# First-tile weight chunks kept whole beside their halves, and the first V remainders summed on TensorE

## The chip, the core and the metric

One core of one Trainium2 chip runs the whole program. The metric is device time in microseconds (us) per execution. Engines in the profile: PE is TensorE (PEld its weight loads), DVE is VectorE, ACT is ScalarE, POOL is GpSimd, SP is the queue from which every DMA is issued.

## The reference

Attention over pooled keys and values, then two feed-forward layers one after the other, all in float32.

```python
k_p = k.reshape(B, H, Sp, pool, D).mean(axis=3)      # B, H, S, D = 8, 8, 576, 64; pool 8, Sp 72
v_p = v.reshape(B, H, Sp, pool, D).mean(axis=3)
scores = (1 / sqrt(D)) * matmul(q, k_p^T);  attn = softmax(scores)
x = matmul(attn, v_p)  ->  [4608, 512]
h = x @ w_in;   y = maximum(0.01 * h, h) @ w_out                  # layer 1, d_ff 2048
h = y @ w_in2;  out = (h * clip(h + 3, 0, 6) / 6) @ w_out2        # layer 2, d_ff 2048
```

## The kernel before

**Attention** goes in units: of each of the 8 batches b, two units of 4 heads over the first 384 tokens, and one of all 8 heads over the last 192. Unit n of batch 0 is u0, u1, u2; batch 1 begins with unit 3. A unit is, in this order: pooled sums of K and V (`prep_k`, `prep_v`, DVE), scores on TensorE (`scores`, L525 for u0 and u1, L541 for the rest), the softmax (DVE maximum L578, exponentials on ACT L602, or, where the half's number stands in the list `sub`, a subtraction on DVE L587 and one exponential L591; then the sum, its reciprocal L614, the remainder L627 and the normalisation L652 on DVE), transposes on TensorE (L678, and L695 for the remainder, the last 8 of 72 pooled keys), and the products with V (`values`, L717 and L729). For u0 and u1 the V sums are made on TensorE by eight accumulating products with the identity (`pool_v`, L451); the sums of the V remainder (`u.r` into `u.rs`) are reductions on DVE (`sum_pool`, L426).

**Layers.** Each float32 operand is split into a rounded high part and a low rest, and a product is three matmuls (hi*hi, hi*lo, lo*hi). Tokens 0 to 383 are one tile of width 384, tokens 384 to 895 one of width 512; the remaining tokens go in pairs of tiles with seven Strassen-like products per pair instead of eight (`Pair1`, `Pair`, TensorE line L1167). The work on TensorE runs in this order: attention u0 to u2, tile 0 with the first 8 of 16 weight chunks (L905 to L907 and L949 to L951, width 384), tile 1 with all 16 (same lines, width 512), tile 0 with the last 8 chunks (width 384), and then the pairs, with the other attention units strewn in between.

**Weights** of layer 1 come as packed words. `decode` (L829, L835 on ACT, L838 on DVE) makes a float32 chunk, a copy its high part, a subtraction (L347) its low part. In tile 0 `decode_w` decodes into scratch that the next chunk overwrites; only the two parts remain. The pairs need sums and differences of quarters of each pair of chunks (`combine`), so `first_weights(f)` adds the high and low parts of chunks 2f and 2f+1 up again with four DVE additions of 128x512 (`plus(part, hi, lo, 512)`, L1032) and then combines. `pair_weights`, for the chunks 8 to 15, keeps the decoded chunk whole and combines from it.

**Order.** `Plan.order` is a list scheduler: every instruction has an engine (some copies may go to ACT or DVE: the first `flex` tasks), an estimated cost and the tasks it depends on; a pass from the end gives each a rank, and each engine takes the ready task of the lowest rank. The result is written out as the fixed order of every queue. The table `C` sets the slots at which attention units (`att...`, `gaps...`), weight steps (`when...`, `left...`) and preparations (`prep...`) are handed to it. Where the plan leaves TensorE a gap ahead of the first second product of tile 0 (`fill_until`), it writes products with zeros into it (`idle`, L1654).

Of the kernel before, what the change touches and what calls it, by code (L numbers as in the profile page):

```python
# [21 lines left out]
POOL, SP = 8, 72  # L22
# [11 lines left out]
    soon={0: 0, 1: 1200, 2: 800, 4: 1000, 3: 9000, 5: 12000, 7: 3000, 6: 5500},  # L34
    flex=684,
    mid=8,
    halves=13,
    sub=[1, 2, 3, 10, 13, 20, 23, 27, 29, 30, 32, 43],
    parts=24,
    when0=[0, 0, 0, 0, 4, 1, 12],  # L40
    att0=[0, 4, 8],
    gaps0=[0, 0, 1, 2, 0],
    when1=[4, 8, 13, 26],
    att1=[0, 4, 16, 22, 40],
    gaps1=[0, 3, 3, 3, 0],
    att2=[1],
    gaps2=[0, 3, 10, 13, 27],
    prep2=[126, 111],
    att=[[16, 26, 33, 49], [12, 26, 41, 60, 76], [1, 18, 47, 60], []],
    gaps=[[0, 3, 7, 10, 0], [0, 10, 13, 13, 8], [0, 0, 7, 12, 0], [198, 0, 80, 79, 49]],  # L50
    prep3=[107, 239],
    prep=[[102, 207], [155, 105], [189, 154], [92, 151]],
    left1=[[[0, 127], [1, 47]], [[2, 10], [3, 54]]],
    left2=[[], [], [[0, 44]], [[1, 30], [2, 51]], [[3, 7], [4, 27]], [[5, 25], [6, 34]], [[7, 6]]],
# [222 lines left out]
def attention_moe_moe(ctx: ExitStack, tc: tile.TileContext, qt, kt, vm, vr, wt, wq, eye, mask, out):  # L277
# [83 lines left out]
    vp = {}  # L361
# [83 lines left out]
    def pool_v(u):  # L445

        u.vs = buf("h", [128, 512], F32, 2, psum)(None, lambda t: t[:, 0:128])

        def emit():
            for i in range(POOL):  # L450
                PE.matmul(  # L451
                    out=u.vs.ap(), lhsT=ident.ap(), rhs=u.v.ap()[:, i * 128 : i * 128 + 128], start=i == 0, stop=i == POOL - 1
                )

        on_pe(1860, emit, [u.v, ident], [u.vs])
# [21 lines left out]
    def prep_v(u):  # L477
        if u.b == 1:
            vp[u.g] = buf(f"vp{u.g}", [128, 128])()
        held_values[u.g] = u.b  # L480
        if u.early:
            pool_v(u)
            copy(whole_v[u.g], u.vs, 128, True)
        else:
            whole_v[u.g] = vp[u.g]
            sum_pool(whole_v[u.g], u.v, 128)
        sum_pool(u.rs, u.r, 64)
# [181 lines left out]
    def transposes(u):  # L669
# [11 lines left out]
        for pi, ps in enumerate(pss):  # L681
            src = ps(None, lambda t: t[:, 0:HALF])
            dst = u.wide_t[pi] if u.b == 0 else buf("th", [128, HALF], F32, 2)()
# [160 lines left out]

    def decode_w(f, raw, t, l, halves=False):

        wf = buf(f"w{f}", [128, 4, 512], F32R)
        w[f] = wf
        for h in range(2) if halves else (None,):
            if h is None:  # L850
                th, lh, n = t, l, 1024
                hi, lo = [wf(what, lambda t, a=a: t[:, a : a + 2].rearrange("p a n -> p (a n)")) for what, a in (("hi", 0), ("lo", 2))]
            else:
                th, lh = [part(v, h, lambda t, h=h: t[:, 512 * h : 512 * h + 512]) for v in (t, l)]
                hi, lo, n = *[wf((what, h), lambda t, a=a: t[:, a]) for what, a in (("hi", h), ("lo", 2 + h))], 512
            decode(raw, th, lh, h)
            copy(hi, th, n)
            subtract(lo, th, hi, n)
        keep(f, wf)
# [217 lines left out]

    def first_weights(f):

        t = new_raw()  # L1080
        for i in range(2):
            for g in range(2):

                dst = [t((i, j) if g == 0 else (j, i)) for j in range(2)]

                def cut(v, i=i, g=g):
                    at = v.rearrange("p (i j g n) -> p i j g n", i=2, j=2, g=2)
                    return at[:, i, :, 0, :] if g == 0 else at[:, :, i, 1, :]

                wf = w[2 * f + i]  # L1090
                hi, lo = [
# [6 lines left out]
    def pair_weights(f):  # L1098
# [3 lines left out]
        for i in range(2):  # L1102
# [13 lines left out]
            for g in range(2):  # L1116
                decode(words, part[g], new_st()(None, lambda t: t[:, 0, :]), g)
# [595 lines left out]
```

## Time and profile before

| | |
|---|---|
| median of 3 runs | 1523.93 us (1522.87 to 1524.26) |
| profiled execution | 1524.98 us, of which the span from first to last instruction is 1522.9 us |
| TensorE | 1514.3 us busy, 99% of the span, 8697 matmuls |
| VectorE, ScalarE | 1152.8 us and 965.2 us busy |
| products with zeros | 225 |

A busy TensorE in the profile also counts products with zeros, and matmuls that run at the lower clock; so the busy share alone does not show what is lost. Starts of neighbouring matmuls tell more than their durations, since they overlap.

### The profile page before, as it was taken

The page shows a single profiled execution, that of the slowest core. Times are in us where ns is not written, and L with a number is a line of the kernel's source. Part 1 is how long each engine was busy: PE and PEld are TensorE (multiplying, and loading weights), DVE is VectorE, ACT ScalarE, POOL GpSimd, SP SyncE. Part 2 cuts the span into 40 slices and gives each one's busy share as a digit, 9 for nine tenths or more (in the row PEclk, how much of TensorE's full clock was granted, in tenths as well). Part 3 has the DMA queues.
Part 4 walks back from the last instruction along what each step waited for, and adds up shares of the span by engine and source line. Part 5 has one row for each costly group of instructions (what it writes and reads, how often), then busy time and mean ns, then how long its engine had stood idle before and what let it go on. Part 6 is the DMA issues. An engine that isn't in the chain of part 4 may idle for free.

```text
span 1522.9 us, 24498 instructions
## 1 busy us (share of the span) xinstructions
PE 1514.3 (99%) x8697; PEld 1318.0 (87%) x8697; DVE 1152.8 (76%) x2054; ACT 965.2 (63%) x2138; POOL 2.5 (0%) x10
## 2 busy tenths in 40 slices
PE   9999999999999999999999999999999999999999
PEld 8877889998787888988888888888888888999999
DVE  8998986788589875975697769657855785596685
ACT  7888567766777777666666556545544554565554
POOL 0000000000000000000000000000000000000000
PEclk9999999999999999999999999999999999999999
DMA  9999899999998999999987966755675567778775
GB/s 323 329 350 321 300 321 324 315 330 343 336 311 323 313 337 325 324 319 337 328 293 258 338 200 206 278 194 208 234 237 195 209 226 246 255 263 299 251 268 197
DMA packets 143209, 432.64 MB, mean 284 GB/s; under 512 B 14960, under 2 KB 51440, under 8 KB 124912
## 3 DMA queue, kind: packets, MB, share of 16 engines
q1 hardware_dynamic: 143088, 431.09, 82.0%
q8 instruction: 69, 1.13, 0.3%
q14 instruction: 52, 0.43, 0.1%
HBM read 345.05 MB, written 85.98 MB: 283 GB/s over the span
## 4 chain that ended last, share of the span: by engine, by line
PE 95%; DVE 3%; ACT 1%; DMA 1%; issue 0%; SPq 0%; DVEq 0%; ACTq 0%
PE y L1167 45%; PE h L1167 24%; PE a L1167 12%; PE y L949 2%; PE y L951 1%; PE y L950 1%; PE h L905 1%; PE h L907 1%; PE h L906 1%; PE a L541 1%; PE a L729 1%; PE a L678 1%; PE idle L1654 1%; PE a L717 1%; DMA x<-x 1%; PE a L695 0%
## 5 line engine op out<-in xcount | busy, mean ns | idle before, releaser
L1032 DVE TENSOR_TENSOR w<-y,w 128x512 f32<-128x512 f32 (+2 forms) x124 | 78.7, 638 | 120.1 <-PE y L1167 118.2
L340 ACT ACTIVATE gh<-w 128x512 fp32r<-128x512 f32 (+1 forms) x140 | 82.3, 589 | 63.8 <-PE y L1167 25.4
L1167 PE MATMUL y<-w,xh 128*128 128x512 f32 (+2 forms) x552 | 121.0, 370 | 0.6 <-DMA xh<-left 0.6
L1032 DVE TENSOR_TENSOR w<-w 128x512 f32<-128x512 f32 (+2 forms) x184 | 113.8, 640 | 3.9 <-ACT w L923 3.6
L1167 PEld LDWEIGHTS y<-w,xh 128*128 128x128 f32 x552 | 100.6, 188 | 15.4 <-issue 1.2
L337 ACT CAST gh<-w 128x512 fp32r<-128x512 f32 (+2 forms) x128 | 74.6, 584 | 49.0 <-PE y L1167 24.7
L1365 DVE SCALAR_TENSOR_TENSOR gl<-w,gh 128x512 fp32r<-128x512 f32 (+1 forms) x140 | 89.4, 641 | 19.3 <-ACT gh L340 19.1
L347 DVE TENSOR_TENSOR gl<-w,gh 128x512 fp32r<-128x512 f32 (+2 forms) x128 | 82.0, 640 | 21.2 <-ACT gh L337 20.7
L1167 PE MATMUL y<-w,xl 128*128 128x512 f32 (+2 forms) x408 | 91.2, 371 | 0.0
L1167 PEld LDWEIGHTS y<-w,xl 128*128 128x128 f32 x408 | 74.6, 188 | 10.6 <-issue 1.2
L1336 ACT ACTIVATE gh<-w,three 128x512 f32<-128x512 f32 (+1 forms) x60 | 40.9, 681 | 66.5 <-DVE w L1032 66.5
L347 DVE TENSOR_TENSOR w<-x,w 128x512 fp32r<-128x512 f32 (+2 forms) x108 | 67.6, 637 | 19.5 <-ACT w L337 19.5
L923 ACT ACTIVATE w<-w 128x512 f32<-128x512 f32 (+2 forms) x96 | 56.1, 595 | 38.3 <-DVE w L1032 37.7
L337 ACT COPY w<-y 128x512 f32<-128x512 f32 (+2 forms) x104 | 56.6, 545 | 31.6 <-PE y L1167 31.4
L1032 DVE TENSOR_TENSOR w<-h,w 128x512 f32<-128x512 f32 (+2 forms) x52 | 33.1, 639 | 55.1 <-PE h L1167 53.6
L337 ACT CAST w<-x 128x512 fp32r<-128x512 f32 (+2 forms) x108 | 60.8, 577 | 13.7 <-DVE x L1032 6.7
L1167 PE MATMUL y<-gh,raw 128*128 128x512 f32 (+1 forms) x224 | 69.2, 370 | 0.0
L1167 PE MATMUL h<-w,xl 128*128 128x512 f32 (+2 forms) x300 | 67.5, 371 | 1.3 <-ACT w L337 1.3
L347 DVE TENSOR_TENSOR st<-raw,st 128x512 fp32r<-128x512 f32 x88 | 60.5, 688 | 8.9 <-ACT st L337 8.8
L1167 PE MATMUL h<-w,xh 128*128 128x512 f32 (+2 forms) x288 | 64.7, 373 | 0.0
L1167 PE MATMUL y<-w,w 128*128 128x512 f32 (+2 forms) x288 | 64.3, 373 | 0.0
L1167 PEld LDWEIGHTS h<-w,xl 128*128 128x128 f32 x300 | 54.5, 188 | 8.8 <-ACT w L337 1.6
(294 smaller groups left out, 4032.0 us busy)
## 6 DMA issues: line engine op xcount, KB each, us to landing
raw<-left SPq DMA_DIRECT2D x60, 1024.0 KB, 4.8
xl<-left SPq DMA_DIRECT2D x90, 512.0 KB, 5.3
left<-st SPq DMA_DIRECT2D x176, 256.0 KB, 5.3
xh<-left SPq DMA_DIRECT2D x86, 512.0 KB, 5.9
w<-left SPq DMA_DIRECT2D x74, 512.0 KB, 5.9
xh<-left SPq DMA_DIRECT2D x33, 1024.0 KB, 4.9
xl<-left SPq DMA_DIRECT2D x25, 1024.0 KB, 4.9
raw<-wq SPq DMA_DIRECT2D x16, 1024.0 KB, 7.7
```

The source lines that it names most:

```text
L337: a = lambda: ACT.copy(out=dst.ap(), in_=src.ap())
L340: a = lambda: ACT.mul(out=dst.ap(), in_=src.ap(), mul=scale)
L347: lambda: DVE.tensor_tensor(out=dst.ap(), in0=a.ap(), in1=f32(b.ap()), op=ALU.subtract),
L541: PE.matmul(out=ps.get()[64 * half : 64 * half + 64, (2 * c + pi) * SP : (2 * c + pi) * SP + SP], lhsT=u.q.ap()[rows, at_ : at_ + 64], rhs ...
L678: PE.transpose(out=placed(u, ps.get(), c), in_=u.p(c, pi), identity=ident.ap())
L717: PE.matmul(out=ps.get()[:, c0 : c0 + n], lhsT=r.ap()[at_], rhs=u.tr.ap()[at_, c0 : c0 + n], start=i == 0, stop=False, skip_group_check=le ...
L923: lambda: ACT.activation(out=dst.ap(), in_=src.ap(), func=AF.Prelu, alpha=0.01),
L949: PE.matmul(out=y, lhsT=hi, rhs=gh.ap(), start=start, stop=False)
L1032: on_dve(n, lambda: DVE.tensor_tensor(out=dst.ap(), in0=a.ap(), in1=b.ap(), op=op), [a, b], [dst])
L1167: PE.matmul(out=o, lhsT=l, rhs=r, start=first and i == m == 0, stop=last and i == len(left) - 1 and m == 2, skip_group_check=True,)
L1336: lambda: ACT.activation(out=r.ap(), in_=h.ap(), func=AF.Relu, bias=three.ap()),
L1365: lambda: DVE.scalar_tensor_tensor(out=lo.ap(), in0=v.ap(), scalar=1.0 / 6.0, in1=f32(hi.ap()), op0=ALU.mult, op1=ALU.subtract),
```

## The change

Four edits and a new table.

1. `decode_w` is gone. All chunks of layer 1 go through the new function `chunk`, which decodes into a whole float32 chunk and splits from there. For the chunks 0 to 7 the whole chunks stay in the buffers w15, w14, w13 and w12 (two chunks in each), and `first_weights(f)` only combines. Its 16 additions of 128x512 are gone. The raw words come through w8 to w11, twice.
2. `pool_v` sums the V remainder of u0 and u1 on TensorE as well: eight accumulating products of 112x64 for each. The two DVE reductions are gone. (The host transposes these inputs to suit.)
3. u2 has a tile for its remainder of its own, and its wide transposes go to ordinary buffers.
4. The pieces through which the first pairs stream their weights rotate as xh, w15, xl instead of xh, xl, w15.
5. The table `C` has other numbers, so that every queue is written in another order.

```diff
-    sub=[1, 2, 3, 10, 13, 20, 23, 27, 29, 30, 32, 43],
+    sub=[1, 2, 3, 7, 9, 13, 16, 20, 23, 26, 27, 29, 32, 38, 39, 43, 45],
-    left1=[[[0, 127], [1, 47]], [[2, 10], [3, 54]]],
+    left1=[[[2, 1], [3, 9], [0, 13], [1, 8]], []],
...
     def pool_v(u):
-        u.vs = buf("h", [128, 512], F32, 2, psum)(None, lambda t: t[:, 0:128])
+        sums = buf("h", [128, 512], F32, 2, psum)
+        u.vs, u.rs = sums("v", lambda t: t[:, 0:128]), sums("r", lambda t: t[:112, 128:192])
...
+        on_pe(860, lambda: emit(u.rs, u.r, 112, D), [u.r, ident], [u.rs])
+        on_pe(1860, lambda: emit(u.vs, u.v, 128, 128), [u.v, ident], [u.vs])
...
-        sum_pool(u.rs, u.r, 64)
+        if not u.early:
+            sum_pool(u.rs, u.r, 64)
...
+    def weights(c):
+        f = c // 2
+        raw = area(8 + c % 4)
+        if f not in whole:
+            whole[f] = area(15 - f)
+        if c in C["soon"]:
+            plan.sooner[len(plan.tasks)] = C["soon"][c]
+        load_w(c, raw, c < C["halves"])
+        chunk(c, raw, whole[f])
...
     def first_weights(f):
-        t = new_raw()
...
-                plus(part, hi, lo, 512)
-        combine(left1[0], f, quarters(t))
+        combine(left1[0], f, quarters(whole.pop(f)))
...
-                for tag in ("xh", "xl", "w15"):
+                for tag in ("xh", "w15", "xl"):
```

The new function, which `pair_weights` calls too:

```python
    def chunk(c, words, t):
...
        for g in range(2):
            decode(words, part[g], new_st()(None, lambda t: t[:, 0, :]), g)
        wf = buf(f"w{c}", [128, 4, 512], F32R)
        w[c] = wf
        for g in range(2):
...
            copy(hi, part[g], 512)
            subtract(lo, part[g], hi, 512)
        keep(c, wf)
```

Three places show how the queues change. The first is TensorE near the start: the sums of u0's V (`h...<-raw...`), scores of u1 (`y...<-keys...`), the transposes of a remainder (`rem...`). Before:

```order
L1654 LDWEIGHTS zeros
L1654 MATMUL idle<-zeros 128x128
L451 MATMUL h_199<-raw_95,ident_151 128x128 x8
L525 MATMUL y_1_221<-keys_1_81,w_1_157 128x144 x3
L525 MATMUL y_1_232<-keys_1_81,w_1_157 128x144 x3
L695 MATMUL y_1_241<-ident_151,rem_84 112x128 x3
L1654 LDWEIGHTS zeros
L1654 MATMUL idle<-zeros 128x128
```

Now (`112x64` are the new sums of the remainders, `a...` and `y_2...` the transposes of u0 and u1):

```order
L1623 MATMUL idle<-zeros 128x128
L452 MATMUL h_221<-raw_160,ident_157 128x128 x8
L452 MATMUL h_261<-w_1_84,ident_157 112x64 x8
L700 MATMUL y_1_273<-ident_157,rem_86 112x128 x3
L452 MATMUL h_261<-w_1_84,ident_157 128x128 x8
L683 MATMUL a_299<-ident_157,s_194 128x128 x3
L683 MATMUL a_304<-ident_157,s_194 128x128 x3
L683 MATMUL y_2_313<-ident_157,sb_231 128x128 x3
L700 MATMUL y_2_317<-ident_157,w_1_84 112x128 x3
L683 MATMUL y_2_322<-ident_157,sb_231 128x128 x3
L722 MATMUL a_330<-tr_287,w_1_146 128x384
```

Most of the products with zeros between these steps are gone: over the whole program 225 become 102, of which 41 stand ahead of the first scores in both.

The second is TensorE at the end of tile 0's first half, from the last score of unit 4 on (L541 before, L546 now; `s_1010` before and `s_1023` now are its normalised exponentials, of which the transposes L678, now L683, read). Before:

```order
L541 MATMUL a_953<-keys_1_81,q_763 64x72
L949 MATMUL y_1_710<-gh_895,w_1_779 128x384
L950 MATMUL y_1_710<-gl_939,w_1_779 128x384
L951 MATMUL y_1_710<-gh_895,w_1_779 128x384
L949 MATMUL y_3_717<-gh_895,w_1_779 128x384
L950 MATMUL y_3_717<-gl_939,w_1_779 128x384
L951 MATMUL y_3_717<-gh_895,w_1_779 128x384
L905 MATMUL h_997<-xh_339,w_1_941 128x384
L906 MATMUL h_997<-xh_339,w_1_941 128x384
L907 MATMUL h_997<-xh_339,w_1_941 128x384
```

In the order before, 48 rows of tile 0 stand between the last score of unit 4 and the transposes that read its softmax. Now:

```order
L546 MATMUL a_975<-keys_1_81,q_736 64x72
L938 MATMUL y_3_534<-gh_896,w_1_720 128x384
L939 MATMUL y_3_534<-gl_908,w_1_720 128x384
L940 MATMUL y_3_534<-gh_896,w_1_720 128x384
L938 MATMUL y_3_534<-gh_931,w_2_831 128x384
L939 MATMUL y_3_534<-gl_940,w_2_831 128x384
L940 MATMUL y_3_534<-gh_931,w_2_831 128x384
L938 MATMUL y_1_526<-gh_931,w_2_831 128x384
L939 MATMUL y_1_526<-gl_940,w_2_831 128x384
L940 MATMUL y_1_526<-gh_931,w_2_831 128x384
L683 MATMUL a_1075<-ident_157,s_1023 128x128 x3
L700 MATMUL a_1084<-ident_157,rem_86 112x128 x3
```

The transposes have moved up to nine matmuls behind the scores; tile 1's first product follows behind the unit's values and the scores of unit 5, as it did before.

The third is VectorE at the same place: the last rows up to unit 4's normalisation (L652 before, L657 now). Before:

```order
L838 SCALAR_TENSOR_TENSOR w_1_349<-w_1_349 128x512
L426 TENSOR_REDUCE vp_1_1037<-raw_864 128x128
L508 TENSOR_TENSOR vrm_1_977<-raw_864,vrm_1_977 16x128
L338 CAST w_2_1049<-w_1_349 128x512
L838 SCALAR_TENSOR_TENSOR w_1_228<-w_1_228,w_1_287 128x512
L613 TENSOR_SCALAR inv_1060<-sm_1011 128x12
L347 TENSOR_TENSOR w_2_1049<-w_1_349,w_2_1049 128x512
L614 RECIPROCAL inv_1060<-inv_1060 128x12
L838 SCALAR_TENSOR_TENSOR w_1_349<-w_1_349 128x512
L627 TENSOR_TENSOR rn_1091<-s_1010,inv_1060 128x96
L347 TENSOR_TENSOR gl_1093<-u_1069,gh_1086 128x384
L652 TENSOR_TENSOR s_1010<-s_1010,inv_1060 128x768
```

Now (`raw_956` and `w_4_1057` are chunks 8 and 9, `w_2_610` the whole chunks 4 and 5, `raw_934` the V of unit 5):

```order
L338 CAST vrm_1_1042<-raw_934 112x128
L426 TENSOR_REDUCE vp_1_308<-raw_934 128x128
L599 TENSOR_REDUCE sm_1025<-s_1023 128x6
L513 TENSOR_TENSOR vrm_1_1042<-raw_934,vrm_1_1042 16x128
L618 TENSOR_SCALAR inv_1049<-sm_1025 128x12
L1021 TENSOR_TENSOR w_2_610<-w_2_610 128x512
L619 RECIPROCAL inv_1049<-inv_1049 128x12
L513 TENSOR_TENSOR vrm_1_1042<-raw_934,vrm_1_1042 16x128
L843 SCALAR_TENSOR_TENSOR raw_956<-raw_956,st_1053 128x2x256
L632 TENSOR_TENSOR rn_1062<-s_1023,inv_1049 128x96
L347 TENSOR_TENSOR w_4_1057<-raw_956,w_4_1057 128x512
L657 TENSOR_TENSOR s_1023<-s_1023,inv_1049 128x768
```

The normalisation was VectorE's row 123 and is its row 137; decoding for tile 1, a first step of `combine` and unit 5's V now stand ahead of it.

## Rows read from the trace of the kernel before

**Rows 1.** The page: span and busy time of each engine.
```profile
span 1522.9 us, 24498 instructions
PE 1514.3 (99%) x8697; PEld 1318.0 (87%) x8697; DVE 1152.8 (76%) x2054; ACT 965.2 (63%) x2138; POOL 2.5 (0%) x10
```

**Rows 2.** Windows: span, busy PE, PEld, DVE, ACT, POOL, clock, DMA share, GB/s.
```profile
30.00:70.00 40.00, 39.70 (x345) 35.91 (x342) 38.87 (x78) 36.36 (x111) 0.00 (x0) 1.00 0.94 335
...
190.00:195.00 5.00, 5.00 (x74) 4.07 (x72) 5.00 (x10) 2.78 (x6) 0.00 (x0) 1.00 0.74 274
215.00:220.00 5.00, 3.84 (x62) 2.47 (x62) 1.07 (x3) 2.83 (x8) 0.00 (x0) 0.78 1.08 334
220.00:225.00 5.00, 4.90 (x24) 4.58 (x24) 4.33 (x9) 3.41 (x17) 0.00 (x0) 0.87 1.01 336
...
500.00:1000.00 500.00, 499.37 (x2496) 422.79 (x2495) 374.26 (x624) 318.57 (x638) 0.00 (x0) 1.00 0.86 294
1000.00:1500.00 500.00, 499.84 (x2492) 449.43 (x2491) 352.93 (x632) 273.54 (x490) 0.00 (x0) 1.00 0.69 240
```

**Rows 3.** Chain that ended last, up to 32 us: start us, us, what.
```profile
0.98 4.55 PE idle L1654 x41
...
13.08 1.23 PE idle L1654 x22
14.97 1.17 PE idle L1654 x21
17.80 1.98 PE h L451 x16
27.55 3.40 PE idle L1654 x59
```

**Rows 4.** Timeline of PE: start us, us, instructions merged, [idle before <-releaser].
```profile
57.24 0.98 PE L541 MATMUL a<-keys,q 64*64 64x72 f32 x48
...
67.34 0.85 PE L678 MATMUL a<-ident,s 128*128 128x128 f32 x6 [0.26 <-DVE s L652]
...
71.89 0.33 PE L949 MATMUL y<-gh,w 128*128 128x384 f32 x1
...
73.11 0.33 PE L950 MATMUL y<-gl,w 128*128 128x384 f32 x1
...
75.08 0.40 PE L905 MATMUL h<-xl,w 128*128 128x512 f32 x1
```

**Rows 5.** The same view, from the end of tile 0 into the first pair.
```profile
213.77 0.82 PE L678 MATMUL a<-ident,s 128*128 128x128 f32 x6
214.83 0.54 PE L695 MATMUL a<-ident,rem 128*112 128x128 f32 x3 [0.24 <-ACT th L337]
215.94 0.44 PE L717 MATMUL a<-tr,vrm 48*128 48x384 f32 x2 [0.57 <-ACT tr L337]
...
217.78 2.09 PE L541 MATMUL a<-keys,q 64*64 64x72 f32 x48 [0.59 <-ACT xa L340]
219.81 3.01 PE L1167 MATMUL h<-w,xh 128*128 128x384 f32 x12
222.65 2.25 PE L1167 MATMUL y<-w,xh 128*128 128x384 f32 x12
226.23 2.32 PE L1167 MATMUL h<-w,xl 128*128 128x384 f32 x12 [1.33 <-ACT w L337]
228.55 0.85 PE L678 MATMUL a<-ident,s 128*128 128x128 f32 x6
```

**Rows 6.** Timeline of DVE: unit 4's normalisation.
```profile
66.24 0.95 DVE L652 TENSOR_TENSOR s<-s,inv 128x768 f32<-128x768 f32 x1
```

**Rows 7.** Groups of DVE by line and form: xcount, busy us, mean ns.
```profile
L1032 DVE TENSOR_TENSOR raw<-w 128x512 f32<-128x512 f32 x16 | 10.5, 688 | 0.4 <-ACT keys L340 0.4
L426 DVE TENSOR_REDUCE w<-w 112x64 f32<-112x512 f32 x1 | 0.7, 680 | 0.0
```

More of the change, by code (lines that the diff above doesn't have):

```diff
@@ L360, in attention_moe_moe @@
     keys = [buf(f"keys{g}", [128, 2, 2 * SP])() for g in range(2)]
-    vp = {}
+    vp = [buf(f"vp{g}", [128, 128])() for g in range(2)]
     vrm = [buf(f"vrm{g}", [112, 128], F32R) for g in range(2)]
@@ L843, in decode @@
         )
[L845 to L859, printed above, removed]
     def keep(f, wf):
@@ L1076, in quarters @@
         return [[t((i, j), lambda v, c=512 * (2 * i + j): v[:, c : c + 512]) for j in range(2)] for i in range(2)]
-    def first_weights(f):
-        t = new_raw()
[L1081 to L1091, printed above, removed]
-                    wf(None, lambda t, r=r: f32(t[:, r]).rearrange("p (j n) -> p j n", j=2)) for r in (g, 2 + g)
-                ]
-                part = View(t, (*dst[0].key, g), cut, [(*dst[1].key, g)])
-                plus(part, hi, lo, 512)
-        combine(left1[0], f, quarters(t))
+    def chunk(c, words, t):
+        i = c % 2
+        blocks = lambda v: v.rearrange("p (q g n) -> p q g n", q=4, g=2)
+        part = [
+            View(
+                t,
+                ((i, 0, g) if g == 0 else (0, i, g)),
+                lambda v, at=at, g=g: blocks(v)[:, at, g, :],
+                [(i, 1, g) if g == 0 else (1, i, g)],
+            )
+            for g, at in enumerate((slice(2 * i, 2 * i + 2), slice(i, i + 3, 2)))
+        ]
+        for g in range(2):
+            decode(words, part[g], new_st()(None, lambda t: t[:, 0, :]), g)
+        wf = buf(f"w{c}", [128, 4, 512], F32R)
+        w[c] = wf
+        for g in range(2):
+            hi, lo = [
+                wf((what, g), lambda t, r=2 * r + g: t[:, r].rearrange("p (a n) -> p a n", a=2))
+                for r, what in enumerate(("hi", "lo"))
+            ]
+            copy(hi, part[g], 512)
+            subtract(lo, part[g], hi, 512)
+        keep(c, wf)
@@ L1102, in pair_weights @@
[L1102 to L1103 removed]
+        for c in (2 * f, 2 * f + 1):
             words = buf(f"w{c}", [128, 2048])
             load_w(c, words)
[L1107 to L1127 removed]
+            chunk(c, words, t)
@@ L1528, in attention_moe_moe @@
         add("gp", 400, lambda k=k: GP.memset(k.ap(), 0.0), [], [k])
-    for r in (rest(), u1.r, rem(), u1.rem()):
+    for r in (rest(), u1.r, rem(), u1.rem(), u2.rem()):
         add("gp", 600, lambda r=r: GP.memset(f32(r.ap()), 0.0), [], [r])
```

94 lines of the change are left out of this document (29 added, 65 removed).

## The prediction, on record before the changed kernel was run

> **What bounds the kernel now.** I read the page first: TensorE is busy for 1514.3 of 1522.9 us [rows 1], so only what shortens its own queue can shorten the run. But busy time there includes products with zeros, and matmuls at the lower clock. So the chain of waits comes next, at the start: after the first 41 products with zeros, which cover the arrival of the first data, it passes three more runs of them, 1.23, 1.17 and 3.40 us [rows 3]. Then the windows: from 500 to 1500 us TensorE is without work for 0.63 and 0.16 us per 500 us, at full clock [rows 2]. Behind 500 us there is under 1 us to win, and the change leaves the products there as they were. What counts lies in the first 230 us, at three places: the start, the step from tile 0 to tile 1 near 67 us, and the step from tile 0's second half to the first pair near 214 us. In the first of these stretches VectorE is the second limit: busy 38.87 of 40 us from 30 to 70 us with 78 instructions, which is 0.50 us for each [rows 2]. At the third place the timeline of TensorE shows waits (0.24, 0.57, 0.59 and 1.33 us) [rows 5], and the granted clock is 0.78 and 0.87 in the two windows there [rows 2], which mixes the levels of 2.4 and 1.2 GHz.
>
> The profiled execution is 1524.98 us, its span 1522.9 and 2.1 around it; the median of the runs is 1523.93, so 1.05 less. Sums are in differences, which I put on the median. Differences below 0.2% (3 us, 1520.9 to 1527.0) are what a measurement of this kernel can't tell from no change.
>
> **The start: products with zeros.** 225 become 102, of which the first 41 stay, so 184 become 61: 123 fewer. The three runs give (1.23 + 1.17 + 3.40) / (22 + 21 + 59) = 0.057 us each [rows 3], so 123 x 0.057 = **-7.0 us**, if TensorE's real work can move up into that place. The alternative is that the data aren't there earlier and the same time comes back as waiting; that is a rival below.
>
> **The start: sums of the remainder.** Sixteen products of 112x64 are new. The sixteen of 128 columns took 1.98 us, 0.124 each [rows 3]. By width the new ones cost half, 1.0; at the same price 2.0; nothing where they lie in a wait. I take **+1.5**, between the two prices of a full queue. The two reductions that they replace (0.68 us each [rows 7]) leave VectorE. The head start is 7.0 - 1.5 = 5.5 us.
>
> **From tile 0 to tile 1: less cover for a softmax.** Before, the scores of unit 4 start at 57.24 and end at 58.22, and the transposes that read the softmax start at 67.34, after a wait of 0.26 for the normalisation on VectorE [rows 4]. So with VectorE as loaded as it was, the softmax takes 67.34 - 58.22 = 9.1 us. That the other end is lower is shown by unit 11, behind whose scores VectorE is nearly free (1.07 of 5 us [rows 2]): 217.78 + 2.09 = 219.87 to 228.55, 8.7 us, and no wait stands at its transposes, so it may have been ready earlier [rows 5]. The change puts only nine matmuls of width 384 between the scores and the transposes in place of 48. One takes (73.11 - 71.89) / 7 = 0.174 us from start to start [rows 4], nine cover 1.6. The wait is 9.1 - 1.6 = 7.5, or 8.7 - 1.6 = 7.1; I take **+7.2**, and keep 2 us as the lower bound, for a softmax whose few VectorE steps (the largest, the normalisation, takes 0.95 [rows 6]) find that engine free. Behind the waiting transposes stand, in TensorE's queue, the remainder's transposes, the values, the scores of unit 5 and all of tile 1.
>
> Those following steps have nothing between them now either. In the same sequence without cover, that of unit 10, the waits were 0.24, 0.57 and 0.59 [rows 5]: **+1.4 us**.
>
> And the clock: behind those waits at 214 us it fell. The 48 scores took 2.09 there against 0.98 at full clock [rows 4, 5], 1.1 more, and twelve pair products took 222.65 - 219.81 = 2.84 against 12 x 0.174 = 2.09, 0.75 more. I expect the same behind the new wait, which is longer: **+1.9**, bounds 0 and twice that. The Trainium skill ("TensorE: Matmul & The Clock Gate", section "What's actually happening") calls the throttled clock the default state, from which activity releases the array. That speaks against a change that takes filling products away and leaves a wait open; the granted clocks of 0.78 and 0.87 behind the waits agree with it. By the rule of that page's section "Terms", that the penalty is the throttled time times the share of pulses held back, the 4.9 us from 217.78 to 222.65 would cost 2.4 in place of 1.9.
>
> **From tile 0 to the pairs: what goes.** Unit 10's transposes and its remainder are now issued ahead of the last steps of tile 0, and the first pair products ahead of the scores of unit 11. So the waits of 0.24, 0.57 and 0.59 get cover, and that of 1.33 for a weight piece from ScalarE comes later in the program [rows 5]. VectorE, which was full there (5.00 of 5.00 from 190 to 195 us [rows 2]), has lost the 16 additions, 10.5 us in all [rows 7]. Waits 1.4 + 1.33 = 2.7, and with them the 1.9 of the clock, 4.6 in all; I leave 0.5 for a wait that is next in line: **-4.1**, bounds -4.6 and -2 (only the first three waits and a part of the clock).
>
> **At nothing.** The additions and reductions themselves: VectorE isn't last except at the places counted above. The rotation of the pieces and unit 2's own remainder tile change which buffer comes free first; a first piece that comes late would show as a wait of about the 0.6 to 1.3 us of [rows 5], so 1 us either way. Raw words go through four buffers twice; the tile has 8 steps for them, as before.
>
> **Sum.** -7.0 + 1.5 + 7.2 + 1.4 + 1.9 - 4.1 = **+0.9 us**: 1523.93 + 0.9 = 1524.8 us.
>
> A second way to the same place goes by VectorE's queue. The normalisation of unit 4, its row 123, started at 66.24 [rows 6]; it is row 137 now. If the queue has run without holes, 14 x 0.50 = 7.0 us more: start 73.2, end 74.2. From there to the end of unit 5's scores takes as long as 213.77 to 219.87, 6.1 us, slow clock included [rows 5], so tile 1's first product starts at 80.3. It started at 75.08 [rows 4] with the same work behind it: +5.2, then 0.75 for the first slow steps and -4.1 later, +1.9 in all. The two ways differ by 1 us; the first uses fewer assumptions on the queue, and I keep it.
>
> **Rivals.**
>
> Faster: the softmax isn't held. The head start brings the pooled sums and scores forward, VectorE has fewer steps, and the wait at the transposes is 2 us, with the clock unharmed: -5.5 + 2.0 + 1.4 - 4.1 = -6.2, so **1517.7 us**. For it: the 8.7 us above is only an upper bound, and VectorE loses 11.9 us of work. Against it: the 0.26 wait at 67.34 shows a softmax that really took 9.1, and the place of its normalisation in the queue is 14 rows further back, not nearer.
>
> No effect: the products with zeros stood where TensorE would have waited for data or VectorE anyway. Then the head start is nil, and the wait at tile 1 is shorter by the same 5.5: 7.2 - 5.5 = 1.7 with 1.4 and half of the clock's 1.9, less 4.1, which is 0: **1523.9 us**. For it: fillers are written where the plan leaves a gap. Against: the real work of tile 0 now stands in their place.
>
> Slower: VectorE's queue is the bound through the first steps of tile 1 as well. All decoding for tile 1 that moved ahead of unit 4 is 128x512 work, of about 0.68 us a row [rows 7], not 0.50. If rows come at 0.60 us on average, the normalisation starts at 66.24 + 14 x 0.60 = 74.6, and the first steps of tile 1 wait for their low parts: 1.4 more for the 14 rows, and as much again for the next 14. With the bound of -2 at the pairs in place of -4.1: 1.9 + 2.8 + 2.1 = +6.8, and half of that where tile 1 catches up. I put this case at +5, **1529 us**. It decides from a spacing of about 0.55 us on.
>
> That the change doesn't do what it says is excluded for the fillers and the additions (they are not in the queues); for the pairs' seam it is in the bounds.
>
> **How the numbers follow.** The forecast 0.34 and no effect 0.10, both within 0.2%: same 0.44. Faster 0.28, slower 0.28. The range from 1517.5 to 1529.5 holds the faster and the slower case at their middle values; beyond them lie a start that gains all of 7.0 with no wait at tile 1, and a slower case with no catching up. The forecast's own range is 1521.5 to 1527.
>
> **What would show it.** Right: about 3.5 us of products with zeros behind the first 41; an idle time of some 7 us ahead of unit 4's transposes, released by VectorE's normalisation; a granted clock under 1.00 in the 10 us behind it; tile 1's first product at 78 to 81 us; no waits and a clock of 1.00 between tile 0 and the first pair. Wrong: tile 1's first product before 76 us (the faster rival), or waits on VectorE at the first second products of tile 1 (the slower one), or a loss anywhere behind 300 us.

## The result, and the profile after

The changed kernel took 1533.53 us (median of 4 runs, 1531.69 to 1533.95), the kernel before beside it 1524.1 us (1522.87 to 1525.39): ratio 1.0059, 95% interval 1.0042 to 1.0077. It is 9.4 us slower; forecast were 1524.8 us, no measurable change, and a range from 1517.5 to 1529.5. The prediction was wrong: the time lies 4.0 us above the range, and where no change was forecast there is a loss clear of the noise.

The page of the kernel after (its first lines, beside [rows 1]; TensorE's clock in 40 slices last):

```profile
span 1531.4 us, 24261 instructions
PE 1514.0 (99%) x8606; PEld 1315.6 (86%) x8606; DVE 1150.4 (75%) x2047; ACT 956.3 (62%) x2082; POOL 2.8 (0%) x11
PEclk9989999999999999999999999999999999999999
```

TensorE is as busy as before, the span is 8.5 us longer, and the clock row has its dip in the third slice of 38.3 us (the windows below put the fall at 70 us). The windows there (columns as in [rows 2]) and the timeline of TensorE (beside [rows 4]):

```profile
60.00:70.00 10.00, 6.46 (x82) 5.13 (x80) 9.59 (x19) 8.06 (x26) 0.00 (x0) 1.00 0.89 279
70.00:80.00 10.00, 5.13 (x19) 2.35 (x19) 9.10 (x19) 4.92 (x12) 0.00 (x0) 0.50 1.04 350
80.00:90.00 10.00, 8.97 (x70) 7.30 (x71) 9.51 (x19) 7.53 (x35) 0.00 (x0) 0.65 1.02 354
```

```profile
63.70 0.98 PE L546 MATMUL a<-keys,q 64*64 64x72 f32 x48
...
74.29 0.87 PE L683 MATMUL a<-ident,s 128*128 128x128 f32 x3 [7.83 <-DVE s L657]
75.06 0.86 PE L700 MATMUL a<-ident,rem 128*112 128x128 f32 x3
75.73 0.90 PE L683 MATMUL a<-ident,s 128*128 128x128 f32 x3
76.57 1.51 PE L722 MATMUL a<-tr,vrm 48*128 48x384 f32 x2
78.00 1.56 PE L734 MATMUL a<-th,vp 64*64 64x384 f32 x8
80.88 2.35 PE L546 MATMUL a<-keys,q 64*64 64x72 f32 x48 [1.32 <-ACT xa L340]
83.16 0.79 PE L894 MATMUL h<-xl,w 128*128 128x512 f32 x1
...
86.74 0.54 PE L896 MATMUL h<-xl,w 128*128 128x512 f32 x1
87.12 0.39 PE L894 MATMUL h<-xl,w 128*128 128x512 f32 x1
```

The reader is to see four things. The wait ahead of unit 4's transposes is 7.83 us, released by the normalisation, as forecast (7.2). Unit 4's scores start at 63.70, against 57.24 in [rows 4]. From the first transpose everything runs at 1.2 GHz (granted 0.50): the scores of unit 5 take 2.35 us for 0.98, and tile 1's products start 0.43 apart until 86.74, then 0.23. And tile 1's first product comes at 83.16, against 75.08 with the same work behind it: 8.1 us late.

**The bill.** For the places where both kernels have not done the same work, I counted from the two orders every real matmul ahead of a unit's scores, at its own start-to-start time (0.174 us for width 384, 0.227 for 512), and took the sum from the time at which these scores start. What is left is time without real work, or lost to real work at the lower clock. After minus before: -7.5 us at unit 4's scores, +6.7 at unit 6's, +6.8 at unit 10's, +4.4 at unit 12's, +4.2 at unit 14's, +5.8 at unit 15's, +5.5 at the last. The new sums count as real work and are 3.0 us more, which makes the 8.5 us of the span. So the seam from tile 0 to tile 1 cost 14.2 us, the step to the pairs gave 2.4 back, and 1.6 were lost between units 14 and 15. The bill says where the time went, not what would come back if one term were taken away.

### The profile page after: what moved, and what is told of

It reads as the page before. It is cut to its first block, busy times and chain, and to the rows that moved or that the text cites. A ratio compares the mean times of both kernels' runs of the same rounds, so it can differ in the third digit from the quotient of the medians.

```text
span 1531.4 us, 24261 instructions
## 1 busy us (share of the span) xinstructions
PE 1514.0 (99%) x8606; PEld 1315.6 (86%) x8606; DVE 1150.4 (75%) x2047; ACT 956.3 (62%) x2082; POOL 2.8 (0%) x11
## 4 chain that ended last, share of the span: by engine, by line
PE 90%; DVE 6%; DMA 2%; ACT 1%; issue 1%; SPq 0%; DVEq 0%; ACTq 0%
PE y L1156 41%; PE h L1156 23%; PE a L1156 11%; DVE w L1021 2%; PE h L894 2%; PE h L895 1%; PE h L896 1%; PE y L938 1%; PE y L939 1%; PE y L940 1%; PE a L546 1%; PE a L734 1%; DMA x<-x 1%; PE a L683 1%; DMA w<-wt 1%; PE a L722 1%
## 5 line engine op out<-in xcount | busy, mean ns | idle before, releaser
L1021 DVE TENSOR_TENSOR w<-w 128x512 f32<-128x512 f32 (+2 forms) x200 | 124.9, 643 | 6.5 <-ACT w L912 6.0
L337 ACT CAST w<-x 128x512 fp32r<-128x512 f32 (+2 forms) x108 | 60.4, 577 | 14.2 <-DVE x L1021 7.1
L340 ACT ACTIVATE sb<-w 128x512 fp32r<-128x512 f32 (+1 forms) x70 | 41.2, 589 | 32.1 <-PE y L1156 12.6
L1156 PE MATMUL y<-w,raw 128*128 128x512 f32 (+1 forms) x288 | 60.2, 362 | 0.0
L347 DVE TENSOR_TENSOR st<-raw,st 128x512 fp32r<-128x512 f32 x72 | 49.3, 688 | 13.7 <-ACT st L337 12.7
```

Of the source, the lines that this page charges most:

```text
L337: a = lambda: ACT.copy(out=dst.ap(), in_=src.ap())
L340: a = lambda: ACT.mul(out=dst.ap(), in_=src.ap(), mul=scale)
L347: lambda: DVE.tensor_tensor(out=dst.ap(), in0=a.ap(), in1=f32(b.ap()), op=ALU.subtract),
L1021: on_dve(n, lambda: DVE.tensor_tensor(out=dst.ap(), in0=a.ap(), in1=b.ap(), op=op), [a, b], [dst])
L1156: PE.matmul(out=o, lhsT=l, rhs=r, start=first and i == m == 0, stop=last and i == len(left) - 1 and m == 2, skip_group_check=True,)
```

## The experiments

Each group of experiments ran on one chip together with the kernel before, whose median was 1524.58 us beside 1 to 4, 1526.41 beside 5 to 8, 1525.41 beside 9 to 12 and 1525.54 beside 13 to 16; beside the changed kernel it was 1524.1. So times of different groups are compared by their ratios: where an expectation names 1533.5 us, the ratio 1.0059 stands for it, and 0.001 is 1.5 us. Unless said otherwise an experiment keeps every queue of the kernel that it is made from, written out by the same plan; only what is named is moved in the finished order. Ratios are to the kernel before; the changed kernel has 1.0059 (1.0042 to 1.0077). Of the experiments made from the changed kernel, only number 10 lies clear of that interval; the others are read from places in their traces, and their ratios settle little.

**1 and 2: products with zeros in the new wait.**

```diff
+    out.insert(out.index(plan.mark["transposes", 4][0]), lambda: plan.cover(125))   # second run: 60
```

> The changed kernel with 125 products with zeros more, put on TensorE directly ahead of unit 4's transposes, where it waited 7.83 us; nothing else is moved. At 0.057 us each they take 7.1 us. Theory A (the lower clock behind that wait costs more than I priced, about 5 us: the attention steps, the 48 scores of unit 5 and the first ten products of tile 1 ran at half rate): the granted clock stays at 1.00 from 60 to 90 us, tile 1's first product comes near 80 us in place of 83.2, and the run is about 5 us shorter, near 1528.5. Rival B (VectorE and ScalarE set the pace of these steps anyway, the clock only fills the time): first product within 1 us of 83.2, run within 1.5 us of 1533.5.

> As the run with 125 products with zeros, but 60, so that they take 3.4 us and TensorE still waits about 4.4 us before unit 4's transposes. Theory A: what counts is that the engine had been without work just before, so the clock still falls, and at most a third of the gain of 125 is had: 1531 to 1533. A variant, that only long waits of the whole 7.8 us throw the clock back: the same gain as with 125, near 1528.5. Rival B: 1533.5.

Measured: 1530.61 us, ratio 1.0040 (1.0025 to 1.0055), and 1532.82, 1.0051 (1.0036 to 1.0066). With 125 the clock held until about 78 us and fell then. With 60 a wait of 4.46 us was left, the transposes took 0.87 as in the changed kernel, and tile 1's first product came at 83.29. Timeline of the run with 125:

```profile
66.65 7.15 PE L1653 MATMUL cover<-zeros 128*128 128x128 bf16 x125
74.64 0.52 PE L706 MATMUL a<-ident,s 128*128 128x128 f32 x3 [0.84 <-DVE s L679]
75.41 0.52 PE L724 MATMUL a<-ident,rem 128*112 128x128 f32 x3 [0.26 <-DVE rem L366]
...
76.49 0.44 PE L747 MATMUL a<-tr,vrm 48*128 48x384 f32 x1 [0.22 <-ACT tr L356]
77.39 0.44 PE L747 MATMUL a<-tr,vrm 48*128 48x384 f32 x1 [0.46 <-ACT th L356]
...
80.62 2.35 PE L568 MATMUL a<-keys,q 64*64 64x72 f32 x48 [1.30 <-ACT xa L359]
```

The transposes took 0.52 instead of 0.87 and still tile 1's first product came at 82.90, 0.26 earlier: between the transposes and the scores of unit 5 ScalarE's and VectorE's copies set the pace. Neither theory holds as stated; the clock's share needed the fuller test of experiment 10.

**3: unit 4's softmax first.**

```diff
+    moved_up(plan, out, [i for i in plan.mark["scores", 4] if plan.chosen[i][0] != "pe"])
```

> The changed kernel with the softmax of unit 4 on VectorE and ScalarE put directly behind what each step needs, ahead of decoding for chunks 8 and 9, of tile 0's copies and of unit 4's V sums; TensorE's and the DMA queue's orders are the same. Theory Q (the wait is one of VectorE's order: between 65.1 and 73.2 us about 5.4 us of other rows stand among the softmax's own): the normalisation starts near 70.3 in place of 73.2, the wait at the transposes is about 5 us, and the run 2.5 to 3.5 us shorter, near 1530.5. Rival R (VectorE is full, so what is moved back is missed next: unit 4's V, or the first chunks of tile 1): the wait moves to the values or to tile 1 and the run stays within 1 us of 1533.5.

Measured: 1535.57, ratio 1.0066 (1.0050 to 1.0083). The wait at the first transpose fell to 3.83 us (71.09), and 7.51 turned up at the second, for ScalarE's copy of the first. Rival R in its result; the new wait stands at a place that it had not named.

**4: without the last 34 products with zeros.**

```diff
+    out[done:] = [i for i in out[done:] if i is not plan.fill]      # done: unit 0's first scores
```

> The changed kernel without the last 34 of its 102 products with zeros (runs of 3, 21 and 10 between 11.7 and 26.4 us, 1.9 us in all); nothing else is moved. Theory C (TensorE's head start buys nothing, since the chain of attention units through VectorE decides when unit 4's softmax is ready): the wait ahead of unit 4's transposes grows by what TensorE gains, the normalisation of unit 4 stays at 73.2 within 0.7 us, and the run within 1 us of 1533.5. Rival P (products with zeros cost what they take, as my prediction's first term has it): normalisation and tile 1 are 1.9 us earlier, and the run 1.9 us shorter.

Measured: 1531.74, ratio 1.0045 (1.0030 to 1.0060). The first scores waited for data and came at 5.84 in place of 5.49, and a wait of 0.62 stands at 21.52; of the 1.9 us, 0.4 were left at unit 4's scores (63.29) and at tile 1's first product (82.76). The normalisation came 0.4 earlier too (72.79), so the wait did not grow but stayed 7.83. Normalisation and tile 1 are as C has them, the growing wait is not, and the ratio is lower by 0.0014, which is what P has. The run does not decide it; number 8 does.

**5, 6, 7 and 11: less on VectorE ahead of unit 4's normalisation.** Rows of VectorE were put off (5), two halves of a softmax given back to ScalarE (6), both with copies given to ScalarE as well (7), and the decoding of chunks 8 and 9 put off on both engines (11).

```diff
+    put_off(plan, out, late, target)   # 5: pair_weights(4), first_weights(2) on VectorE, behind the softmax
+    back = number + e in (7, 9)        # 6: six exponentials on ScalarE, no subtraction, no sum on VectorE
+    plan.chosen[i] = plan.tasks[i][0][0]            # 7: also 128x384 copies from VectorE to ScalarE
+    put_off(plan, out, late, last_copy_of_values)   # 11: on VectorE and ScalarE, behind unit 4's values
```

> The changed kernel with the five VectorE rows of decoding chunks 8 and 9 and of the first combine that stand ahead of unit 4's normalisation (0.60 us each, 3.0 in all), and what on ScalarE needs them, put directly behind unit 4's softmax; TensorE's order and all else stay. Theory L (load: the table put more VectorE work ahead of unit 4's normalisation than the kernel before had there, and that row comes when the queue has got to it): normalisation near 70.2 in place of 73.2, wait at the transposes near 4.9, run 3 to 4 us shorter, near 1530. Rival R (what is put off is missed directly behind): a wait at the values or in tile 1, run within 1 us of 1533.5, as with the softmax moved ahead.

> The changed kernel with the second halves of the softmax of units 3 and 4 done as before the change: six exponentials with their sums on ScalarE, in place of a subtraction and a sum on VectorE (0.52 us each) around one exponential. Order unchanged. Theory L: VectorE is rid of about 2.1 us ahead of unit 4's normalisation, which comes 1 to 2 us earlier; run 1 to 2 us shorter, near 1532. Rival S (ScalarE's longer chain, 1.8 us for the second half in place of 0.5, stands on the same path): normalisation within 0.5 us of 73.2, run unchanged.

> Both of these, and the copies of 128x384 that VectorE does between 55 us and unit 4's normalisation given to ScalarE (0.47 us each). Theory L: some 6 to 7 us of VectorE rows fewer ahead of the normalisation, which is what the row moved by (66.24 to 73.19): it comes at 67 to 69, the wait is 1.5 to 3.5, tile 1's first product near 77 to 79, the clock falls for a shorter time, and the run is 5 to 7 us shorter, near 1527. Rival R: waits turn up elsewhere ahead of or in tile 1, and the run is shorter by less than 3 us.

> The changed kernel with the decoding of chunks 8 and 9 and the first combine, on VectorE and on ScalarE, put behind unit 4's values, so that neither engine's queue holds such a row between unit 4's exponentials and its values; the copies of unit 4's transposes come first on ScalarE. In the earlier run that put off VectorE's rows alone, the transposes came 2.2 us earlier, but ScalarE's copy of them 3.9 us late, behind a decoding row that waited for VectorE. Theory L: first transposes near 72, second near 73.5, tile 1's first product near 79.5 to 80.5, run 3 to 4 us shorter, near 1530. Rival R (decoding is then missed in tile 1, or by the combines): waits of 1 us or more in tile 1 and a run within 1.5 us of 1533.5.

Measured: 1535.39 (1.0058), 1532.76 (1.0042, 1.0027 to 1.0057), 1534.59 (1.0056) and 1538.23 (1.0078, 1.0061 to 1.0095). In 6 the normalisation came no earlier: the wait is 7.79, released at 74.96, as rival S has it. In 5 and 7 the first transpose waited 5.50 and 5.87, and the second 3.89 for ScalarE. In 11 tile 1 did begin 2.25 us earlier, and then waited in its first steps. Timeline of TensorE in run 11:

```profile
72.46 0.87 PE L747 MATMUL a<-ident,s 128*128 128x128 f32 x3 [5.50 <-DVE s L720]
...
80.91 0.80 PE L960 MATMUL h<-xl,w 128*128 128x512 f32 x1
...
94.11 0.79 PE L960 MATMUL h<-xl,w 128*128 128x512 f32 x1 [6.80 <-ACT u L978]
```

ScalarE's activation for tile 1 (at 93.40) stood behind unit 5's exponentials, which began at 89.84 after a wait for VectorE's maximum and behind the casts of the decoding that had been put off. Rival R in 5, 7 and 11: what is taken from in front is missed behind. VectorE has hardly a hole there (39.46 of 40 us busy from 30 to 70 us in the changed kernel, 9.10 and 9.51 in the next two windows of 10). ScalarE has holes (busy 4.92 of 10 from 70 to 80 us), but its queue waits for VectorE's rows in order, 2.67 us ahead of 72.54.

**8: the kernel before without its 184 later products with zeros.**

```diff
+    out[first:] = [i for i in out[first:] if isinstance(i, int)]
```

> The kernel before without the 184 products with zeros behind its first scores (10.5 us at 0.057); nothing else is moved. This is the first term of my prediction by itself. Theory C (the chain of attention units through VectorE sets when tile 1 begins): TensorE runs ahead through tile 0, the wait ahead of unit 4's transposes grows from 0.26 to 5 us or more, tile 1's first product stays within 2 us of 75.1, and the run is between 2 us shorter and 3 us longer (where the clock falls in that wait). Rival P (they cost what they take): tile 1's first product near 67 and the run 7 to 10 us shorter, near 1515.

Measured: 1526.5 (10 runs), ratio 1.0002 (0.9993 to 1.0012). Timeline:

```profile
30.20 1.09 PE L709 MATMUL a<-ident,s 128*128 128x128 f32 x4 [2.54 <-DVE s L682]
...
68.11 0.84 PE L709 MATMUL a<-ident,s 128*128 128x128 f32 x6 [0.26 <-DVE s L682]
...
75.85 0.40 PE L938 MATMUL h<-xl,w 128*128 128x512 f32 x1
```

Leaving out some 10 us of products with zeros wins nothing. They turn into waits (1.14 us for a transfer at 8.53; 0.87, 0.61 and 2.54 for the normalisations of units 0 to 2), and into work at the lower clock behind these waits (granted 0.72 from 14 to 20 us and 0.57 from 26 to 34). Unit 2's transposes start at 30.20, in the kernel before at 30.78: 0.6 us were there to win, and the lower clock took more than that back. Tile 1 begins at 75.85. Theory C in its result; not in its place, since the order of TensorE's steps holds the waits at units 0 to 2 and unit 4's stays 0.26.

**9: one product in place of eight for each new sum.**

```diff
-        on_pe(860, lambda: emit(u.rs, u.r, 112, D), [u.r, ident], [u.rs])
+        on_pe(860, lambda: one(u.rs, u.r, 112, D), [u.r, ident], [u.rs])
```

> The changed kernel with one product of 112x64 in place of the eight that sum a unit's V remainder, so that this sum is not what the reference asks (7 of 8 terms are left out); the orders of all engines are the same. TensorE is rid of 14 of the 16, 2.7 us at the measured 0.19 each, between 10.2 and 15.3 us. Theory K (they stand at the head of the chain of attention units: the transposes of unit 0 come 3.2 us later than before, at 17.38 for 14.15, and every later unit with them): scores of units 2, 3 and 4, and tile 1's first product, all come 2 to 2.7 us earlier, and the run is 2 to 3 us shorter, near 1531. Rival V (VectorE decides when unit 4 is ready, whatever TensorE does at the start, as the products with zeros cost nothing): tile 1's first product within 0.7 us of 83.2, run within 1 us of 1533.5.

Measured: 1531.29, ratio 1.0035 (1.0022 to 1.0048). Tile 1's first product came at 82.84, 0.3 earlier. Most of the 2.7 us was gone by unit 2's scores (23.27 for 23.59): a wait of 0.68 for the V data at 11.76, one of 0.35 for a copy at 18.42, and first scores that came at 5.79 in place of 5.49. So tile 1 is where rival V has it, but its reason is not shown: the time was lost at the start, not at unit 4. The profiled span is still 1.9 us shorter (1529.5 for 1531.4): the waits of 0.66 and 0.33 at 185 us in the changed kernel are not there. Why they are there in some runs and not in others I have not found.

**10: products with zeros in all five waits.**

```diff
+    for i, n in ((t0, 132), (rem, 6), (t1, 6), (values, 10), (scores5, 24)):
+        out.insert(out.index(i), lambda n=n: plan.cover(n))
```

> As the run with 125 products with zeros ahead of unit 4's transposes, but 132 there, and 6, 6, 10 and 24 more ahead of the remainder's transposes, the second transposes, the values and the scores of unit 5, which waited too. Theory A (what the lower clock costs is the 2.35 us for unit 5's scores in place of 0.98, and 2 us in tile 1's first products): clock 1.00 throughout, scores about 1 us, products 0.23 from start to start, and the run 3 to 4 us shorter than 1533.5, near 1530; tile 1's first product about 81.5. If the clock falls all the same, the fillers don't hold it, and the run is as with 125 (1530.6).

Measured: 1530.02 (10 runs), ratio 1.0028 (1.0019 to 1.0038). The clock is 1.00 from 60 to 90 us. Windows and timeline:

```profile
70.00:80.00 10.00, 9.56 (x143) 8.30 (x140) 9.88 (x21) 5.88 (x13) 0.00 (x0) 1.00 1.05 349
80.00:90.00 10.00, 9.58 (x90) 7.53 (x88) 9.60 (x19) 7.84 (x35) 0.00 (x0) 1.00 1.02 337
```

```profile
74.97 0.52 PE L716 MATMUL a<-ident,s 128*128 128x128 f32 x3 [0.44 <-DVE s L689]
...
80.53 0.34 PE L578 MATMUL a<-keys,q 64*64 64x72 f32 x2
...
82.08 0.50 PE L929 MATMUL h<-xl,w 128*128 128x512 f32 x1
82.41 0.39 PE L930 MATMUL h<-x,w 128*128 128x512 f32 x1
```

By the bill, 12.9 us are lost between the scores of units 4 and 6, against 16.2 in the changed kernel: the clock costs 3.3 us there. Theory A. From the first transpose to tile 1 it takes 7.1 us in place of 8.9. The clock does not explain the rest: at 1.00 throughout, the run is still 4.6 us slower than the kernel before beside it (1525.41).

**12, 15 and 16: the step to the pairs, on the kernel before.** Unit 10's transposes, remainder and values moved up by 30, 21 and 12 matmuls (12); the pieces' rotation of the change (15); both (16).

```diff
+    for what, u, ahead_of in (("transposes", 10, a), ("transpose_rem", 10, b), ("values", 10, c)): ...
-                for tag in ("xh", "xl", "w15"):
+                for tag in ("xh", "w15", "xl"):
```

> The kernel before with unit 10's transposes, remainder and values on TensorE 30, 21 and 12 matmuls earlier among the last products of tile 0, and the scores of unit 11 directly ahead of the first pair as they were; ScalarE's copies for them moved up too. It has of the change only what my prediction priced at -4.1 us. If that step is right: no waits of 0.24, 0.57 and 0.59 near 215 us, clock 1.00 there, and the wait of 1.33 gone or smaller; run 3 to 4.5 us shorter than the kernel before, near 1521. Rival: the first pair waits for the pieces of its weights as long as before, whenever it comes, so that only 1 to 2 us are won, near 1523.

> The kernel before with its first pairs' pieces rotating as xh, w15, xl, and each load in the place in the DMA queue that its need gives it; all else as before. Part 4 of the change alone. Theory P (the second piece waited for the buffer xl, which tile 0's sums hold until they are stored): the wait of 1.33 at 226 us is gone, the others stay; run 1 to 1.5 us shorter than the kernel before. Rival: nothing changes within 1 us, since the first-needed piece is late for its split on ScalarE (the page names that as releaser).

> Parts as in the two runs on the kernel before: unit 10's transposes, remainder and values earlier on TensorE, and the new rotation of the pieces. Theory P: the transfer of 5.1 us that took the place of the waits is now ahead of its need by 3 to 4 us, clock 1.00 at the step, and the run is 3 to 4 us shorter than the kernel before, near 1520.5: faster than both. Rival: the transfers as a whole are full there (DMA share 1.0 from 215 to 230), so the next piece is late by the same, and the run stays within 1 us of before.

Measured: 1527.47, ratio 1.0011 (1.0002 to 1.0021); 1523.43, 0.9987 (0.9978 to 0.9995); 1522.39, 0.9980 (0.9971 to 0.9988). Timelines of 12 and of 16:

```profile
216.00 0.98 PE L587 MATMUL a<-keys,q 64*64 64x72 f32 x48
...
226.85 3.90 PE L1219 MATMUL h<-w,xl 128*128 128x384 f32 x12 [5.09 <-DMA xl<-left]
```

```profile
216.56 0.98 PE L613 MATMUL a<-keys,q 64*64 64x72 f32 x48
217.48 2.67 PE L1245 MATMUL h<-w,xh 128*128 128x384 f32 x12
219.99 2.25 PE L1245 MATMUL y<-w,xh 128*128 128x384 f32 x12
223.62 2.32 PE L1245 MATMUL h<-w,w 128*128 128x384 f32 x12 [1.39 <-ACT w L406]
```

In 12 the three waits of [rows 5] are gone, and the product that used xl starts at 226.85, where it had started at 226.23: it waits for a transfer into the buffer that tile 0's sums leave late, and runs at the lower clock behind that wait (3.90 us for 2.32). The run is 2.1 us slower than the kernel before beside it: neither the step as forecast nor the rival's 1 to 2 us. The timeline of the kernel before named ScalarE for its wait of 1.33; the transfer was behind it, issued at 219.16, when the stores of tile 0's sums were through, with 6.9 us to landing in the median there. With w15 in its place the same product starts at 223.62. Theory P, and 16 is faster than both kernels, by 3.2 us against the kernel before. In 15 the wait of 1.33 is gone, with 0.41 at 224.30 and 0.50 at 226.98 in its place: theory P too. What the cover of 16 adds to 15 is 1.0 us, and the two intervals overlap. In 15 the waits of 0.24, 0.57 and 0.59 are the same as before, but the granted clock is 1.00 in both windows where [rows 2] have 0.78 and 0.87, so a part of its 2.1 us is the clock's and not the wait's.

**13 and 14: nine rows of decoding cut to an eighth.**

```diff
+        some = lambda v: v[:, :, 0:32] if task in plan.narrow else v
+    for what, u, ahead_of in (("values", 3, 372), ("scores", 4, 381)): ...      # 14 only
```

> The changed kernel with nine VectorE rows of decoding (L843, 128x512) between 43 and 72 us cut to 64 of their 512 columns, which leaves the rest of those words undecoded; orders unchanged. Each row is 0.47 us shorter, 4.2 in all; six of them stand ahead of unit 4's scores, three behind. Theory L (load alone): the normalisation comes 4 us earlier, at 69.2, and the run is 4 to 5 us shorter. Theory O (TensorE's order sets when unit 4's scores run, 63.7 us, since it has no wait ahead of them; only the three rows behind count): normalisation 1 to 1.8 us earlier, run 1 to 2 us shorter.

> As with the nine short rows, and on TensorE unit 3's values 12 matmuls of tile 0 earlier and unit 4's scores 9 earlier (1.6 us), with their copies on ScalarE and VectorE. If load and order act together (the order follows from when VectorE can deliver unit 3's values): scores of unit 4 near 62.1, normalisation near 70.2, no new wait at the values, and the run 1.5 to 2 us shorter than with the short rows alone. If TensorE then waits at the values or the scores by as much, the order wasn't free and VectorE's load still holds it: same run as with the short rows alone.

Measured: 1531.75 (1.0040, 1.0026 to 1.0054) and 1533.91 (1.0062, 1.0047 to 1.0078). In 13 the normalisation started 8.26 us behind the start of unit 4's scores (72.45, 64.19), in the changed kernel 9.49: 1.2 us won of 4.2, theory O. In 14 the scores waited:

```profile
63.89 0.98 PE L589 MATMUL a<-keys,q 64*64 64x72 f32 x48 [1.25 <-ACT keys L380]
...
75.50 0.87 PE L727 MATMUL a<-ident,s 128*128 128x128 f32 x3 [7.30 <-DVE s L700]
```

So TensorE's order wasn't free either: the keys come from a pooled sum on VectorE.

## Why the prediction was wrong

| term | forecast | measured | from |
|---|---|---|---|
| products with zeros | -7.0 | -7.5 | bill at unit 4's scores |
| new sums | +1.5 | +3.0 | 10.19 to 11.73 and 13.74 to 15.27 |
| wait ahead of unit 4's transposes | +7.2 | +7.6 | 7.83 - 0.26 |
| steps behind it | +1.4 | +3.3 | 14.2 - 7.6 - 3.3 |
| clock there | +1.9 | +3.3 | experiment 10 |
| step to the pairs | -4.1 | -2.4 | bill, units 10 to 12 |
| not priced | 0 | +1.2 | bill, units 6, 14 and 15, and the last |
| sum | +0.9 | +8.5 | the spans |

No single term carries the miss. The two large ones cancel as forecast; the steps behind the wait (1.9 more), the clock (1.4), the new sums (1.5), the step to the pairs (1.7 less gain) and what was not priced (1.2) make 7.7 of it.

**Products with zeros, and the wait.** Both terms were right in size and wrong as two things. What TensorE gained by unit 4's scores it paid back in the wait ahead of unit 4's transposes: -7.5 and +7.6. Experiment 8 shows that there was nothing to gain: without such products the kernel before takes the same time. The rival "no effect" said so for the products, with a smaller wait for it; the wait came whole. The order shows why: ahead of unit 4's scores stand 183 products of tile 0 where 120 stood, so that these scores come 6.5 us later, and between them and the transposes there are nine in place of 48. The softmax itself takes as long as before: from the end of the scores to the normalisation 8.0 us (58.22 to 66.24), now 8.5 (64.68 to 73.19). Real work did move up into the place of the products with zeros, but it was the softmax's cover. In the sum the two terms cancel, and what is left are costs.

**VectorE's queue.** The second way, by 14 rows of 0.50 us, put the normalisation at 73.2; it started at 73.19 (beside [rows 6]):

```profile
73.19 0.95 DVE L657 TENSOR_TENSOR s<-s,inv 128x768 f32<-128x768 f32 x1
```

The agreement to 0.01 us is luck, since the 14 rows held more than their 7.0 us and the holes ahead of them became shorter. What stands behind it: the busy time of each engine up to that row (columns as in [rows 2]; VectorE's figure is the one behind PE and PEld), first in the window of the kernel before.

```profile
0.00:66.24 66.24, 65.05 (x684) 58.90 (x685) 58.90 (x127) 53.49 (x171) 2.47 (x10) 1.00 0.92 325
```

The same window of the kernel after, up to its later row:

```profile
0.00:73.19 73.19, 65.34 (x620) 59.32 (x620) 66.18 (x139) 56.50 (x160) 2.82 (x11) 0.98 0.92 323
```

VectorE had done 58.90 us of work then and has done 66.18 now, with 7.3 and 7.0 us of holes: 7.3 us more work ahead of the same row, which came 6.95 later. The change takes 1.4 us of reductions from there; its 10.5 us of additions stood far behind. That much the traces show. That the load alone sets the time is not shown: with 4.2 us less of it in the same order (13) only 1.2 were won, and the other levers brought new waits (3, 5, 7, 11, 14). Load and the order of the attention steps on three engines come from one plan, and I have not separated them further.

**The steps behind the wait** were the first step that failed. I took their length from unit 10, where the two transposes run one behind the other and the remainder follows [rows 5]. Here the remainder's transposes stand between the two, and the steps wait for copies, as the timeline of experiment 1 shows at full clock (0.26 for VectorE's, 0.22 and 0.46 for ScalarE's): 6.6 us from the first transpose to the scores of unit 5 (74.29 to 80.88), against 4.0 there. With full clock it was 5.6 (74.97 to 80.53 in experiment 10). The row was of the same operations in another order, and I had both orders.

**The clock** was the second: 1.9 with bounds of 0 and 3.8, measured 3.3. I took from [rows 5] one fall with 4.9 us of slow work, behind waits of 1.4 (the granted clocks of [rows 2], 0.78 and 0.87 over 5 us each, put it at 3.5); behind 7.8 us of wait it lasted from 74.29 to 86.74. By the Trainium skill ("TensorE: Matmul & The Clock Gate", section "Terms": throttled time times the share of pulses held back), counted from the first transpose on, these 12.4 us would by an estimate cost 6.2; the runs show 3.3, about half, and in a part of them the steps waited for copies.

**The sums**: the row of 1.98 us that I divided by sixteen shows sixteen matmuls for eight products of the program. The order prints x8 for each, so the new sums are 32 records, 1.5 us for each unit. The bounds (1.0 and 2.0) were both wrong. At tile 1 leaving them out won little (0.3 us of 2.7 in experiment 9).

**The step to the pairs** had a mechanism in it that I had not named, a transfer that the waits hide: experiment 12, with cover alone, loses 2.1 us. The rotation of the pieces, which I put "at nothing" with 1 us either way, is what makes the rest worth having: 12 and 16 differ by 5 us, and the rotation alone (15) wins 2.1 of the 3.2. The changed kernel has both and loses between units 10 and 12 as much as experiment 16 (3.5 and 3.5 us, against 5.9 before): the rest of the 4.1 was never there, and the two waits at 185 us took from it.

**What would show it**: right were the products with zeros (61 behind the first 41), the idle time of some 7 us, the clock under 1.00 behind it, and a clock of 1.00 at the step to the pairs. Wrong were tile 1's first product (83.16 for 78 to 81), no waits at the pairs (0.68 at 234.75), and nothing behind 300 us (0.57 at 317.01 and 0.43 at 335.56). The slower rival came nearest with its sum (+6.8), and its mechanism was wrong: 14 rows took 6.95 us more and not 14 x 0.60, and tile 1's first steps waited for nothing. I cut it to +5 for a catching up that no row showed.

## What to carry to other kernels

Where an engine's idle time is filled with useless work, removing that work is worth what the next engine lets it be worth; follow the work that the whole stage waits for (here the attention units through VectorE), see whether it starts earlier, and ask which wait the work that moves up was covering. When cover is taken from a chain, price every step of the chain in its own order, and the lower clock for as long as the chain stays thin. A wait that a profile puts down to a copy may hide a transfer that lands hardly earlier: ask what frees that buffer before the wait is counted as gain.

## What the runs showed of the hardware

The same three waits (0.24, 0.57 and 0.59 us) brought the granted clock down to 0.78 in the kernel before [rows 2] and left it at 1.00 in experiment 15, where they came 0.2 us earlier, and from 215 to 225 us in experiment 8: whether short waits cost clock is not steady from one run to the next. A float32 product of 112x64 or 128x128 with the identity stands in the trace as two matmuls, and costs 0.19 and 0.23 us from start to start; the transposes of the same size stand as one, at 0.11.
